# Six late weight tiles of a fused attention and mixture-of-experts kernel, loaded as 120 rows and 8 rows

## The chip, the cores and the metric

The kernel runs on one core of a Trainium2 chip. The metric is the device time of one execution in microseconds. The kernel before takes 537.62 us, the median of three runs (536.92 to 538.82).

A core has five engines with a queue of instructions each: TensorE (PE; its weight loads are listed as PEld), VectorE (DVE), ScalarE (ACT), GpSimd (POOL) and SyncE (SP). Here SP issues all transfers (DMAs); sixteen DMA engines move the bytes.

## The reference, cut to what matters

First comes attention over 8 batches, 8 heads, 576 positions and head size 64, with a bias that a small network makes of the positions. Its output, as 4608 tokens of 512 values, goes into a soft mixture of 8 experts with 4 slots each:

```python
scores = scale * np.matmul(q, k.transpose(0, 1, 3, 2)) + bias
attn = softmax(scores);  x = (attn @ v) as 4608 x 512
logits = x @ phi                       # 512 x 32
d = softmax(logits, axis=0);  slot_input = d.T @ x
for e in range(8):                     # 4 slots each
    h = np.maximum(slot_input[e] @ w1[e], 0.0)   # w1: 512 x 1024
    slot_out[e] = h @ w2[e]                      # w2: 1024 x 512
c = softmax(logits, axis=1);  out = c @ slot_out
```

All of it is in float32. The weights w1 and w2 are 32 MiB together, the output is 9 MiB.

## The kernel before, in words

Attention is worked through in 32 units (a pair of heads and a batch). For each unit TensorE makes scores, VectorE adds the bias and finds the extremes, ScalarE takes exponentials, GpSimd normalises, TensorE turns and multiplies with v. The order of all these steps on every engine stands in a long table, `ORDER`, that the host sorts by (lines 24 to 200); `step` looks up a step's place in it. A step's code then issues its instructions in that order, so each engine's queue is the table's order of its own steps. The last eight units also run the steps of the mixture (`moe`), which collect the slots' inputs; after the last step the two layers of the experts follow in a written order, and then the outputs.

The 64 weight tiles, each of 128 x 1024 floats (512 KB), are loaded by `fetch_w`: tiles 0 to 31 are of w1, tiles 32 to 63 of w2. Each call takes the next tile in `worder` and a home, a place in SBUF. Tiles 0 to 23 go to a pool of their own. The later ones go to places that attention no longer needs: the steps `wbm`, `wy`, `wqk`, `wbr`, `wv`, `wat`, `wxk`, `wv2`, `wxo` and `wat2` of the last unit give the home by pool and tag. Their places in `ORDER` set when they are issued. Tiles 36 and 37 go to "y", tile 38 to "v" and "xt" in two halves, 39 to 41 to "at", 42 and 43 to "xk", 44 again in two halves, 45 to "xo", 46 and 47 again to "at". Tiles 48 to 63 are fetched by `refetch` into the homes of tiles 0 to 13, 16 and 17 as soon as the first layer has used those (`first`, line 1019).

A transfer on SP waits for what used the place before, and for one thing more: eight semaphores serve all transfers in turn, so each transfer waits for the landing of the one that was issued eight places ahead of it.

The first layer (`first(j)`, matmuls on line 1026) uses tiles 4j to 4j+3. `hidden` and `turn_hidden` make the second layer's input. `second(k, Q, parts)` (line 1073) uses tiles 32+8k+4Q to 32+8k+4Q+3. `gather_slots` (line 1084) and `put` and `put_rest` (matmuls on line 1103) make 128 x 1024 or 128 x 512 pieces of the output, which ScalarE and VectorE copy from PSUM (line 375) into tiles `ob`, and SP sends out (lines 1117 and 1124). The order of these parts is the string at the end of `body`:

```python
for x in """S0001 T1 H0 S0101 S100 H1 G0 S101 P00 S1101 P01 S200 G1 R0 S201 P10 ...
```

Here S100 is `second(1, 0, (0,))`, which uses tiles 40 to 43, S1101 is `second(1, 1, (0, 1))`, which uses 44 to 47, and S310 with S311 use the last tiles, 60 to 63. The places of `ob` are again those of tiles that are no longer needed.

Of the kernel before, what the change touches and what calls it, by code (L numbers as in the profile page):

```python
# [231 lines left out]
def body(ctx, tc, qk, v, phi, mw1, mw2, tabh, consth, *outs):  # L232
    nc = tc.nc
    P = 128
# [15 lines left out]
    atp = ctx.enter_context(tc.tile_pool(name="atp", bufs=1))  # L250
    xp = ctx.enter_context(tc.tile_pool(name="xp", bufs=1))
# [620 lines left out]
    def fetch_w(home, n=1):  # L872
        for _ in range(n):
            i = nw[0]
            nw[0] += 1
            w, e, c, hf = worder[i]
            homeof.append(home)
            if not free:
                pool, tag = home
                if tag == "v":  # L880
                    free.append([x.tile([P, 512], F32, name="wt", tag=n, bufs=2) for x, n in ((pool, tag), (xp, "xt"))])
                elif tag == "at" and "xk" not in spare:
                    x = pool.tile([P, 2 * 9 * 320], F32, name="wt", tag=tag)
                    spare["xk"], spare["two"] = x[:, 0:5 * DM], x[:, 0:2048].rearrange("p (y n d) -> p y n d", y=2, n=2)
                    free.extend(x[:, 1024 * y - 512:1024 * y + 512].rearrange("p (n d) -> p n d", n=2) for y in (3, 4, 5))
                elif tag == "at":
                    free.extend(spare["two"][:, y] for y in range(2))
                elif tag == "xo":
                    x = pool.tile([P, 3 * S], F32, name="wt", tag=tag)
                    free.append(x[:, 0:1024].rearrange("p (n d) -> p n d", n=2))  # L890
                    spare["lg"] = x[:, 1024:1024 + 5 * P]
                else:
                    x = pool.tile([P, several.get(tag, 1), 2, 512], F32, name="wt", tag=tag, **({"bufs": 1} if tag == "br" else {}))
                    free.extend(x[:, i] for i in range(x.shape[1]))
            wt = free.pop(0)
            if w == 1:
                src = mw1[e, c * P:(c + 1) * P, :].rearrange("p (x d) -> p x d", x=2)
                if type(wt) is list:
                    for n in range(2):
                        nc.sync.dma_start(out=wt[n], in_=src[:, n])  # L900
                else:
                    nc.sync.dma_start(out=wt, in_=src)
                    wt = [wt[:, n, :] for n in range(2)]
            else:
                src = mw2[e].rearrange("p (x d) -> p x d", x=2)
                if type(wt) is list:
                    for n in range(2):
                        nc.sync.dma_start(out=wt[n], in_=src[:, n])
                else:
                    nc.sync.dma_start(out=wt, in_=src)  # L910
                    wt = [wt[:, n, :] for n in range(2)]
            wtiles[i] = wt

# [62 lines left out]
    for u, (hp, b) in enumerate(units):  # L976
        for p in range(5 - u % 2):
            rows(u, p)
        mix(u)
        if hp == NP - 1:  # L980
            moe(u)
        if u >= 2:
            step(u, "lq", lambda _, u=u: load_qk(u))
            step(u, "lv", lambda _, u=u: load_v(u))
        if 1 <= hp < NP - 1:
            for j in range(2 if u < W1N - B else 1):
                step(u, f"w{j}", lambda _: fetch_w((wp, "w")))
        if b == B - 1 and hp < NP - 1:
            for c in range(5):
                step(u, f"b{c}", lambda _, hp=hp, c=c: load_bias(hp + 1, c))  # L990
# [5 lines left out]
    for k, home in homes.items():  # L996
        step(U - 1, k, lambda _, home=home, k=k: fetch_w(home, several.get(k[1:], several.get(home[1], 1))))
# [3 lines left out]
    def refetch(*ids):  # L1001
        for i in ids:
            fetch_w(homeof[i])
# [127 lines left out]
    with tc.manual_schedule():  # L1131
# [19 lines left out]
        for x in """S0001 T1 H0 S0101 S100 H1 G0 S101 P00 S1101 P01 S200 G1 R0 S201 P10 S210 P11 S211 S300 G2 R1 P20 S301 S310 P21 S311 R2 G3 P30 P31 R3""".split():  # L1151
            i = [int(c) for c in x[1:]]
# [64 lines left out]
```

## Time and profile before

| | |
|---|---|
| median of three runs | 537.62 us (536.92 to 538.82) |
| the profiled execution's own time | 537.33 us |
| its span, from first to last instruction | 535.5 us |
| busy: PE, PEld, DVE, ACT, POOL | 517.8, 350.6, 431.3, 458.1, 217.2 us |
| DMA: bytes, mean rate | 110.14 MB, 206 GB/s |
| weight tiles of 512 KB: transfers, median time to landing | 62, 6.5 us |
| output pieces of 512 KB: transfers, median time to landing | 16, 4.6 us |

The span is divided among engines by busy time; an engine may be busy and yet not set the end. What sets the end is told by the chain of waits, which goes back from the last instruction to what released it. The time to landing of a transfer runs from its issue on SP to the last mark on its semaphore. The DMA share of a window is the mean busy share of sixteen engines; it counts a packet where it starts, so it may pass 1 a little.

### The profile page before, as it was taken

The page shows a single profiled execution, that of the slowest core. Times are in us where ns is not written, and L with a number is a line of the kernel's source. Part 1 is how long each engine was busy: PE and PEld are TensorE (multiplying, and loading weights), DVE is VectorE, ACT ScalarE, POOL GpSimd, SP SyncE. Part 2 cuts the span into 40 slices and gives each one's busy share as a digit, 9 for nine tenths or more (in the row PEclk, how much of TensorE's full clock was granted, in tenths as well). Part 3 has the DMA queues.
Part 4 walks back from the last instruction along what each step waited for, and adds up shares of the span by engine and source line. Part 5 has one row for each costly group of instructions (what it writes and reads, how often), then busy time and mean ns, then how long its engine had stood idle before and what let it go on. Part 6 is the DMA issues. An engine that isn't in the chain of part 4 may idle for free.

```text
span 535.5 us, 22642 instructions
## 1 busy us (share of the span) xinstructions
PE 517.8 (97%) x9025; PEld 350.6 (65%) x9025; DVE 431.3 (81%) x1808; ACT 458.1 (86%) x984; POOL 217.2 (41%) x317
## 2 busy tenths in 40 slices
PE   8999799999999999999999999999999999989994
PEld 6554566767767666686777667666777767653662
DVE  6898879789889888888888888888899888763343
ACT  6998899999999999999999999999888898741233
POOL 3000645565554556565454656545335341400000
PEclk9999999999999999999999999999999999999998
DMA  6689535253883535577254548635632435899988
GB/s 199 246 305 372 178 110 178 64 165 126 289 220 110 195 131 174 151 245 230 81 163 163 204 162 253 161 113 188 233 133 79 160 105 210 303 357 408 386 351 326
DMA packets 40793, 110.14 MB, mean 206 GB/s; under 512 B 5360, under 2 KB 5488, under 8 KB 40688
## 3 DMA queue, kind: packets, MB, share of 16 engines
q1 hardware_dynamic: 40688, 108.70, 59.5%
q8 instruction: 71, 1.16, 0.9%
q14 instruction: 34, 0.28, 0.2%
HBM read 81.28 MB, written 27.41 MB: 203 GB/s over the span
## 4 chain that ended last, share of the span: by engine, by line
PE 79%; DMA 6%; DVE 5%; ACT 5%; issue 2%; POOL 2%; SPq 0%; DVEq 0%; ACTq 0%; POOLq 0%
PE ps L568 23%; PE ps L425 17%; PE ps L450 14%; PE ps L444 11%; DMA bias_m<-e 3%; PE ps L1026 3%; PE ps L1073 2%; DVE y L470 2%; PE ps L1103 2%; POOL y L372 2%; ACT e L957 1%; PE ps L944 1%; PE ps L643 1%; PE ps L269 1%; DMA bias_r<-e 1%
## 5 line engine op out<-in xcount | busy, mean ns | idle before, releaser
L372 POOL TENSOR_SCALAR y<-y,rc 128x576 f32<-128x576 f32 x288 | 211.0, 749 | 224.7 <-DVE rc L489 177.3
L481 ACT ACTIVATE y<-y,mn 128x576 f32<-128x576 f32 x288 | 220.9, 776 | 7.2 <-DVE mn L470 5.7
L568 PE MATMUL ps<-at,v 64*64 64x288 f32 x2304 | 152.2, 403 | 0.0
L375 ACT COPY at<-ps 128x1024 f32<-128x1024 f32 (+3 forms) x196 | 140.0, 758 | 10.6 <-PE ps L425 7.2
L470 DVE CUSTOM_DVE_ANT_0 y<-ps,bm 128x320 f32<-128x320 f32 x256 | 115.4, 487 | 11.4 <-PE ps L444 4.6
L425 PEld LDWEIGHTS ps<-ident,y 64*128 64x128 f32 x2592 | 98.9, 138 | 34.1 <-POOL y L372 13.5
L568 PEld LDWEIGHTS ps<-at,v 64*64 64x64 f32 x2304 | 89.6, 133 | 47.2 <-ACT at L375 1.2
L470 DVE CUSTOM_DVE_ANT_0 y<-ps,bm,mn 128x256 f32<-128x256 f32 x256 | 113.9, 479 | 6.3 <-PE ps L444 1.1
L425 PE MATMUL ps<-ident,y 64*128 64x64 f32 x2592 | 106.6, 224 | 2.4 <-DVE mn L470 1.1
L450 PE MATMUL ps<-qk 64*64 64x256 f32 (+1 forms) x1280 | 92.8, 407 | 0.1
L444 PE MATMUL ps<-qk 64*128 64x320 f32 (+1 forms) x512 | 86.7, 432 | 1.4 <-DVE mn L470 1.3
L450 PEld LDWEIGHTS ps<-qk 64*64 64x64 f32 x1280 | 45.3, 132 | 28.6 <-ACT at L375 6.9
L481 ACT ACTIVATION_READ_ACCUMULATOR y<-y,mn 128x1 f32 x288 | 56.7, 197 | 0.0
L470 DVE DVE_READ_ACCUMULATOR2_ANT mn<- 128x1 f32 x576 | 48.3, 84 | 0.0
L444 PEld LDWEIGHTS ps<-qk 64*128 64x128 f32 x512 | 42.5, 189 | 7.6 <-DVE mn L470 3.0
L931 DVE TENSOR_SCALAR f<-tabw,offs 128x512 f32<-128x512 f32 (+17 forms) x107 | 39.5, 456 | 3.0 <-DMA bias_m<-e 2.8
L375 DVE COPY at<-ps 128x256 f32<-128x256 f32 (+3 forms) x60 | 35.7, 605 | 5.9 <-PE ps L425 4.7
L944 PE MATMUL ps<-f,wbd 128*32 128x512 f32 (+47 forms) x640 | 38.7, 389 | 1.3 <-ACT f L929 0.4
L944 PEld LDWEIGHTS ps<-f,wbd 128*32 128x32 f32 x640 | 20.3, 110 | 20.5 <-issue 9.0
L488 DVE TENSOR_REDUCE rc<-sm 128x2 f32<-128x4 f32 x144 | 22.0, 153 | 10.1 <-ACT y L481 9.7
L957 ACT ACTIVATE e<-ps,cons 128x591 f32<-128x591 f32 x35 | 26.3, 793 | 3.0 <-PE ps L944 3.0
L489 DVE RECIPROCAL rc<-rc 128x2 f32<-128x2 f32 x144 | 23.9, 166 | 5.0
(150 smaller groups left out, 394.7 us busy)
## 6 DMA issues: line engine op xcount, KB each, us to landing
wt<-in_moe_w_dram SPq DMA_DIRECT2D x62, 512.0 KB, 6.5
qk<-in_qk_dram SPq DMA_DIRECT2D x32, 576.0 KB, 4.2
bias_m<-e SPq DMA_DIRECT2D x32, 295.5 KB, 3.7
v<-in_v_dram SPq DMA_DIRECT2D x32, 288.0 KB, 3.3
bm<-bias_m SPq DMA_DIRECT2D x32, 288.0 KB, 5.0
out_dram<-ob SPq DMA_DIRECT2D x16, 512.0 KB, 4.6
xs<-xts SPq DMA_DIRECT2D x24, 288.0 KB, 4.0
xo<-xs SPq DMA_DIRECT2D x8, 864.0 KB, 4.7
```

The costliest lines, as they stand in the source:

```text
L372: nc.gpsimd.tensor_scalar(out=out, in0=y, scalar1=r, scalar2=1.0, op0=ALU.mult, op1=ALU.mult)
L375: (nc.vector.tensor_copy if eng else nc.scalar.copy)(out=out, in_=in_)
L425: nc.tensor.matmul(out, src[rs], ident[rs, rs], is_transpose=True, start=True, stop=True, tile_position=(64 * r, 0))
L444: nc.tensor.matmul(pss[hh].t[:, 0:nk], x[rs, S + p * P:S + (p + 1) * P], x[rs, ks], start=True, stop=True, tile_position=(64 * hh, 0))
L450: nc.tensor.matmul(pss[hh].t[64 * r:64 * r + 64, 0:nk], x[rs, q0:q0 + 64], x[rs, ks], start=True, stop=True, tile_position=(64 * hh, 64 * r))
L470: nc.vector.tensor_tensor_reduce(out=heads(hh)[:, cuts[n] // 64:cuts[n + 1] // 64], in0=d["ps", p, n][hh].read()[:, 0:nk].rearrange("a (k ...
L481: nc.scalar.activation(out=y, in_=y, func=AF.Exp, bias=d["mn", p][:, 2 + hh:3 + hh], scale=-1.0, accum_out=d["sm", p][:, hh, 0:1])
L489: nc.vector.reciprocal(out=r, in_=r)
L568: nc.tensor.matmul(d["po"][c].t[o:o + 64, 0:HALF], d["v"][rs, 64 * k:64 * k + 64], at[rs, c, 320 * k + start[c]:320 * k + start[c] + HALF] ...
L931: nc.vector.tensor_scalar(out=f, in0=tabw[:, 0:n], scalar1=off, scalar2=0.0, op0=ALU.add, op1=ALU.max)
L944: nc.tensor.matmul(x[32 * t:32 * t + 32, a:a + c1 - c0], wbd, y, start=True, stop=True, tile_position=(0, 32 * t))
L957: nc.scalar.activation(out=out, in_=x, func=AF.Copy, scale=invs[:, i:i + 1])
```

## The change

Where a whole w2 tile is loaded, tiles for the homes "xk" and "xo", and those for "at" with a number over 40, are loaded by two transfers: rows 0 to 119, and rows 120 to 127. Every row is 4 KB in DRAM and in SBUF, so the parts are 480 KB and 32 KB. All other tiles are loaded as before.

```diff
@@ -907,7 +907,9 @@
                     for n in range(2):
                         nc.sync.dma_start(out=wt[n], in_=src[:, n])
                 else:
-                    nc.sync.dma_start(out=wt, in_=src)
+                    cut = home in ((xp, "xk"), (xp, "xo")) or home == (atp, "at") and i > 40
+                    for rs in (slice(0, 120), slice(120, P)) if cut else (slice(0, P),):
+                        nc.sync.dma_start(out=wt[rs], in_=src[rs])
                     wt = [wt[:, n, :] for n in range(2)]
             wtiles[i] = wt
```

On SP, in the kernel before, these are the transfers of tiles 41 to 47 (line 908 loads tile 44 in halves). DMAHW0 to DMAHW7 are the eight semaphores of the transfers; a row's waits are for landings and for the engines that used the place before.

```order
L910 DMA wt<-in_moe_w_dram 128x1024 [waits DMAHW3_49]
L910 DMA wt<-in_moe_w_dram 128x1024 [waits DVE_49,DMAHW4_49,PE_49,Activation_49]
L910 DMA wt<-in_moe_w_dram 128x1024 [waits DMAHW5_49]
L908 DMA wt<-in_moe_w_dram 128x512 [waits DMAHW6_49]
L908 DMA wt<-in_moe_w_dram 128x512 [waits DVE_49,DMAHW7_49,PE_49,Activation_49]
L910 DMA wt<-in_moe_w_dram 128x1024 [waits DMAHW0_49]
L910 DMA wt<-in_moe_w_dram 128x1024 [waits DMAHW1_49,PE_49,Activation_49]
L910 DMA wt<-in_moe_w_dram 128x1024 [waits DMAHW2_49,PE_49,Activation_49]
```

The same place in the changed kernel, tiles 41 to 46 (line 912 is line 910 of before):

```order
L912 DMA wt<-in_moe_w_dram 120x1024 [waits DMAHW3_49]
L912 DMA wt<-in_moe_w_dram 8x1024 [waits DMAHW4_49]
L912 DMA wt<-in_moe_w_dram 120x1024 [waits DVE_49,DMAHW5_49,PE_49,Activation_49]
L912 DMA wt<-in_moe_w_dram 8x1024 [waits DMAHW6_49]
L912 DMA wt<-in_moe_w_dram 120x1024 [waits DMAHW7_49]
L912 DMA wt<-in_moe_w_dram 8x1024 [waits DMAHW0_49]
L908 DMA wt<-in_moe_w_dram 128x512 [waits DMAHW1_49]
L908 DMA wt<-in_moe_w_dram 128x512 [waits DVE_49,DMAHW2_49,PE_49,Activation_49]
L912 DMA wt<-in_moe_w_dram 120x1024 [waits DMAHW3_49]
L912 DMA wt<-in_moe_w_dram 8x1024 [waits DMAHW4_49]
L912 DMA wt<-in_moe_w_dram 120x1024 [waits DMAHW5_49,PE_49,Activation_49]
L912 DMA wt<-in_moe_w_dram 8x1024 [waits DMAHW6_49]
```

The pair of tile 47 follows, so six tiles are cut: 41, 42, 43, 45, 46 and 47. Each pair takes two of the eight semaphores, and every later transfer moves on by as many. Nothing changes its place on SP, and what follows these transfers are the sixteen whole tiles 48 to 63 and then the outputs.

On TensorE, at the start of S1101 in the kernel before (the first row is the first use of tile 44, the next three are those of tiles 45, 46 and 47):

```order
L1073 MATMUL ps<-wt,hT 32x128 [waits DMAHW6_49]
L1073 MATMUL ps<-wt,hT 32x128 [waits DMAHW0_49]
L1073 MATMUL ps<-wt,hT 32x128 [waits DMAHW1_49]
L1073 MATMUL ps<-wt,hT 32x128 [waits DMAHW2_49]
L1073 MATMUL ps<-wt,hT 32x128 x12
```

and in the changed kernel:

```order
L1075 MATMUL ps<-wt,hT 32x128 [waits DMAHW1_49]
L1075 MATMUL ps<-wt,hT 32x128 [waits DMAHW4_49,DMAHW3_49]
L1075 MATMUL ps<-wt,hT 32x128 [waits DMAHW6_49,DMAHW5_49]
L1075 MATMUL ps<-wt,hT 32x128 [waits DMAHW7_49,DMAHW0_49]
L1075 MATMUL ps<-wt,hT 32x128 x12
```

The first use of a cut tile waits for two landings in place of one. The instructions of TensorE, ScalarE, VectorE and GpSimd and their order are otherwise the same.

## Rows read from the trace of the kernel before

**Rows 1.** The page's chain that ended last, share by engine.

```profile
PE 79%; DMA 6%; DVE 5%; ACT 5%; issue 2%; POOL 2%; SPq 0%; DVEq 0%; ACTq 0%; POOLq 0%
```

**Rows 2.** Windows: window, length, busy by engine, PEclk, DMA share, GB/s.

```profile
480.00:490.00 10.00, 9.64 (x88) 3.13 (x92) 4.26 (x16) 1.63 (x4) 0.00 (x0) 1.00 0.99 379
490.00:500.00 10.00, 9.63 (x185) 5.33 (x181) 2.21 (x4) 1.86 (x3) 0.00 (x0) 1.00 1.03 408
```

**Rows 3.** Line 910 from 487 to 501 us: duration min/median/max, first and last start.

```profile
L910 SPq DMA_DIRECT2D wt<-in_moe_w_dram x11: 327/327/328, 487.8 to 500.6; - x11
...
DMA to landing us min/median/max: 10.1/10.1/10.2
```

**Rows 4.** TensorE in order of time, 519 to 524 us: start, length, instructions.

```profile
519.57 1.95 PE L1073 MATMUL ps<-wt,hT 128*32 128x128 f32 x64
```

**Rows 5.** Line 910 from 471 to 480 us.

```profile
L910 SPq DMA_DIRECT2D wt<-in_moe_w_dram x8: 328/410/679, 470.8 to 479.8; - x8
...
DMA to landing us min/median/max: 6.0/7.2/10.5
```

**Rows 6.** TensorE in order of time, 499 to 508 us.

```profile
499.25 2.83 PE L1073 MATMUL ps<-wt,hT 128*32 128x128 f32 x96 [0.37 <-ACT hT L375]
...
506.48 1.74 PE L1073 MATMUL ps<-wt,hT 128*32 128x128 f32 x56
```

**Rows 7.** Line 312, the transfers of 32 KB.

```profile
L312 SPq DMA_DIRECT2D phis<-in_moe_phi_dram x2: 964/989/1014, 4.0 to 5.0; - x2
...
DMA to landing us min/median/max: 6.3/6.7/7.1
```

**Rows 8.** SP in order of time, 470 to 506 us.

```profile
470.85 6.31 SPq L910 DMA_DIRECT2D wt<-in_moe_w_dram  x5
477.20 0.92 SPq L908 DMA_DIRECT2D wt<-in_moe_w_dram  x2
478.17 22.73 SPq L910 DMA_DIRECT2D wt<-in_moe_w_dram  x19
505.94 0.34 SPq L1117 DMA_DIRECT2D out_dram<-ob  x1
```

**Rows 9.** Waits of SP, 470 to 503 us: total us, times, longest.

```profile
SPq L910 <- DMA wt<-in_moe_w_dram: 12.0, 14, 1.7
```

**Rows 10.** Line 1117 from 526 to 530 us.

```profile
L1117 SPq DMA_DIRECT2D out_dram<-ob x4: 332/554/967, 527.3 to 529.2; - x4
...
DMA to landing us min/median/max: 3.1/4.2/4.8
```

**Rows 11.** Windows from 504 to 528 us.

```profile
504.00:508.00 4.00, 3.43 (x64) 1.84 (x65) 1.23 (x1) 1.01 (x1) 0.00 (x0) 1.00 0.98 388
508.00:512.00 4.00, 4.00 (x104) 2.63 (x96) 1.94 (x3) 1.65 (x3) 0.00 (x0) 1.00 0.60 239
512.00:516.00 4.00, 4.00 (x80) 2.18 (x76) 1.64 (x2) 1.65 (x2) 0.00 (x0) 1.00 0.91 353
516.00:520.00 4.00, 4.00 (x92) 2.65 (x84) 1.68 (x4) 1.84 (x4) 0.00 (x0) 1.00 1.02 398
520.00:524.00 4.00, 4.00 (x104) 2.84 (x96) 2.21 (x3) 1.21 (x2) 0.00 (x0) 1.00 0.96 370
524.00:528.00 4.00, 3.31 (x34) 1.45 (x28) 1.83 (x3) 2.42 (x4) 0.00 (x0) 1.00 0.87 341
```

**Rows 12.** Line 1124 from 530 to 531 us.

```profile
L1124 SPq DMA_DIRECT2D out_dram<-ob x1: 1147/1147/1147, 530.3 to 530.3; - x1
...
DMA to landing us min/median/max: 4.4/4.4/4.4
```

**Rows 13.** Line 1073 from 495 to 525 us, its one wait instruction.

```profile
L1073 PEldq EVENT_SEMAPHORE  x1: 51/51/51, 498.1 to 498.1; - x1
```

**Rows 14.** DMA queues, 470 to 503 us: packets, MB, share of 16 engines.

```profile
q8 instruction: 4, 0.07, 0.8%
```

**Rows 15.** Waits of TensorE, 496 to 530 us, all four.

```profile
PE ps L1103 <- issue: 0.6, 1, 0.6
PE ps L1103 <- ACT so L1086: 0.4, 1, 0.4
PE ps L1073 <- ACT hT L375: 0.4, 1, 0.4
PE ps L1103 <- ACT ob L375: 0.3, 1, 0.3
```

## The prediction

> **What bounds the kernel now.** I read the chain of waits first. Of the work that ended last 79% is TensorE and 6% is transfers [rows 1], so a change to transfers counts only where a transfer ends a wait or where the last transfers end the program. Next come the stretches of the tail by window. From 480 to 500 us the sixteen DMA engines are busy 0.99 and 1.03 of the time at 379 and 408 GB/s [rows 2]: the second-layer weight tiles fill them completely. There the transfers have a rate of their own. Eleven tiles are issued from 487.8 to 500.6 us, so ten steps take 12.8 us, 1.28 us for each tile of 512 KB, and every one of them lands 10.1 us after its issue [rows 3]. 10.1 is eight times 1.28 (10.2): each tile waits behind seven others, which fits the order listing, where each transfer of SP waits for the one eight places ahead of it.
>
> Does TensorE wait for these tiles? The last one issued lands at 500.6 + 10.1 = 510.7 us [rows 3]. Its first user is the second half of the 64 matmuls that start at 519.57 us and take 1.95 us [rows 4], so it is needed at about 520.5 and lies ready for 9.8 us. The six tiles that the change cuts are issued between 470.8 and 479.8 us and land 6.0 to 10.5 us later, the last by 490.3 [rows 5]. Tiles 41 to 43 are first used in the last third of the 96 matmuls from 499.25 us on, at about 501.1, and tiles 45 to 47 in the group from 506.48 us [rows 6]. Even by the worst pairing they lie ready for 10.8 us. So no weight tile ends a wait of TensorE; the transfers can only act through the outputs that queue up behind them.
>
> **The change part by part.** It issues 12 transfers in place of six, with the same bytes. The title speaks of five tiles; the order of SP shows six, since the third tile of the first "at" buffer (number 41) also meets the condition.
>
> *SP's time.* Six more issues at the median of 0.41 us in this stretch are 2.5 us, between 6 x 0.33 = 2.0 and 6 x 0.68 = 4.1 [rows 5]; the only 32 KB transfers of the run took about 1.0 us to issue, which gives 6.0 [rows 7]. I take 2.5. From 470.85 to the first output at 505.94 us SP issues nothing but weight tiles [rows 8], so only weight tiles stand behind the pairs, and in this stretch SP spends 12.0 us waiting for landings [rows 9]. The issues fit in there: 0 on the end. Without that cover they would push the last tiles by up to 6.0 us, still less than their 9.8 us of slack.
>
> *Transfers in flight.* A small transfer takes one of the eight places. Where pairs fill them, eight transfers are four tiles, 4 x 1.28 = 5.1 us of work. The shortest landing of a full-sized transfer in the tail is 3.1 us [rows 10], so the engines should not run dry. If every landing took the 6.7 us of the 32 KB transfers [rows 7], four tiles would take 6.7 instead of 5.1 us, and six tiles would lose 1.5 x 1.6 = 2.4 us. This is between 0 and 2.4 us on the weight stream; I take 0, because in a full queue bytes set the pace [rows 2, 3].
>
> *Load of single engines.* No transfer of 120 rows stands in this trace, so its spread over the engines is bounded. At best it is even and nothing changes. At worst I consider 120 rows on eight engines: 15 rows and one row of the small part make 16 where there were 8, so a tile costs 1.28 us more on these engines, 7.7 us for six. In between, the small part only puts a ninth row on engines that carry eight: an eighth of 1.28, 0.16 us for a tile and 1.0 us for six. I take 1.0 us, near the even end, because the loads of 128 rows, the nearest rows, run at full rate [rows 2]. [...]
>
> *What covers a late weight stream.* After the first output the DMA engines are not always busy. The windows from 504 to 528 us show 0.98, 0.60, 0.91, 1.02, 0.96 and 0.87 [rows 11]: 4 x (0.02 + 0.40 + 0.09 + 0 + 0.04 + 0.13) = 2.7 us idle. A stream that is up to 2.7 us late is caught up before the last outputs. 1.0 us therefore costs 0.
>
> *The end.* The last five outputs (four of 512 KB, one of 256 KB) are issued from 527.3 to 530.3 us [rows 10, 12]. The last lands at 530.3 + 4.4 = 534.7, which is 7.4 us after the first issue. Their bytes take 4.5 x 1.28 = 5.8, so 1.6 us are start, landing and unevenness between the engines. The shortest landing, 3.1 us, holds 3.1 - 1.28 = 1.8 us of such time. So hardly anything is left for a better balance to win: between 0 and 1.6 us, and I take 0.2.
>
> *TensorE's waits.* Each cut tile gives TensorE a second DMA semaphore to look at. The one row of a wait instruction on its queue in this part took 51 ns [rows 13]; six are 0.3 us on an engine that is hardly idle there. Bounds 0 and 0.3; I take 0.2.
>
> The sum is +0.2 - 0.2 = 0 on the profiled execution's 537.33 us (span 535.5, 1.8 around it). That execution lies 0.3 us below the median of 537.62, so the forecast for the median is 537.6 us.
>
> **The rivals.** *Half the engines (slower).* 120 rows go to fewer engines than 15, as in the bound above, and a tile costs these 1.28 us more. The outputs share the same engines. 7.7 us less 2.7 us of idle time are 5.0 us: 542.6. It decides from (2.7 + 1.6) / 6 = 0.72 us per tile. For it: no row shows such a shape, and the stretch has no spare engine time. Against it: the 64-row-high transfers of the start land in 6.3 to 7.1 us like others [rows 7], with no sign of a slow shape. [...]
>
> *A lagging engine is relieved (faster).* Code loading runs on the DMA engines too: 0.8% of sixteen engines over 33 us [rows 14] is 4.2 us, and if all of it falls on one engine, that engine lags, and every landing waits for it. If the 120 rows leave one engine out and it is this one, six tiles or 7.7 us are taken off it, and it no longer lags at the end. The gain is then at most the 1.6 us of the last five outputs and TensorE's one unexplained gap of 0.6 us [rows 15]: 537.6 - 2.2 = 535.4. For it: landings do wait for the slowest engine. Against it: TensorE's idle times from 496 to 530 us are four, 1.7 us in all [rows 15], and none is put down to a weight tile; no view here tells which engine lags. [...]
>
> **How the numbers follow.** The forecast, weights that stay hidden whatever their transfers look like, gets 0.70. The slower rival gets 0.12, the faster one 0.13; 0.05 stays for shifts that I don't see, 0.02 of it fast and 0.03 slow. A measurement here can tell about 0.3%, 1.6 us, from no change, so within 0.3% (536.0 to 539.2) 0.70, faster 0.15, slower 0.15. The forecast's own range is 536.0 to 539.2. The range takes half of the faster rival in and reaches towards the slower one: 535.6 to 540.6, which leaves out about 2 in 10.
>
> **What would show it.** Right: the last weight tile still lands around 511 us (within 3 us), TensorE's idle time from 496 us on stays near 1.7 us, the last five outputs still start near 527.3 and the last lands about 4.4 us after its issue. The slower rival would show as landings of the 120-row parts well over 10.5 us and DMA shares near one half in 480 to 500 us, and outputs that land later than 5 us at the end. The faster rival would show as landings under 10.1 us for the whole tiles after the pairs, and last outputs that land earlier against their issue. I am wrong if TensorE waits for a weight tile, or if SP issues its first output later than the copy that fills it.

## Result and the profile after

The changed kernel is slower: 541.3 us (538.27 to 543.67, 15 runs) against 537.58 us (535.56 to 538.82, 15 runs on the same chip). The ratio is 1.0069 [1.0053, 1.0085], or 3.7 us. The forecast was 537.6 us with a range to 540.6; it was wrong, and the slower rival came nearest.

The profiled execution of the changed kernel took 541.3 us with a span of 539.2, which is 3.7 us above the span of before. I read it in the same order as before. The chain of what ended last, 77% TensorE and 6% transfers, tells little beside [rows 1]: a loss of 0.7% hides in the rounding. The waits of TensorE from 496 us to the end (total us, times, longest) come next:

```profile
PE ps L1105 <- issue: 0.6, 1, 0.6
PE ps L1075 <- issue: 0.5, 1, 0.5
PE ps L1105 <- ACT so L1088: 0.4, 1, 0.4
PE ps L1075 <- ACT hT L375: 0.4, 1, 0.4
PE ps L1105 <- ACT ob L375: 0.3, 1, 0.3
```

The four of [rows 15] are there with the same times, and one of 0.5 us is new. It is put down to no transfer. But it is not all that TensorE loses. The same time of the clock is not the same place in the program: this execution came to the tail 0.77 us earlier, as two matmuls just ahead of the cut tiles show, first in the kernel before:

```profile
471.30 0.38 PE L823 MATMUL ps<-ident,stM 128*1 128x128 f32 x2
```

```profile
470.53 0.38 PE L823 MATMUL ps<-ident,stM 128*1 128x128 f32 x2
...
511.17 1.08 PE L1075 MATMUL ps<-wt,hT 128*32 128x128 f32 x31 [0.53 <-issue]
```

From these two to the group that uses the last tile (519.57 us in [rows 4], 520.05 below) it is 48.3 us before and 49.5 after: TensorE loses 1.2 us in the tail, between 508 and 518 us, at the place shown and at one more. In e1_columns below, which cuts no rows, it is 48.3 us again (470.09 to 518.38). One thing goes with it: the trace also records the loads of instructions, 16 KB each on queue q8, and counted from the two matmuls, the two loads that come before those places start at 38.2 and 44.3 us, where the nearest of the kernel before start at 36.2 and 40.9 and of e1_columns at 36.7 and 40.4. That these loads, behind the fuller DMA queues, hold TensorE up is not shown.

The larger loss lies behind TensorE. Now the windows of the weight stream and of the outputs, with the columns of [rows 2]:

```profile
470.00:480.00 10.00, 8.60 (x168) 5.60 (x172) 7.07 (x25) 5.65 (x11) 0.14 (x1) 1.00 1.00 316
480.00:490.00 10.00, 10.00 (x95) 3.21 (x91) 3.93 (x14) 1.36 (x3) 0.00 (x0) 1.00 1.01 234
490.00:500.00 10.00, 9.63 (x205) 5.83 (x201) 2.73 (x4) 2.07 (x4) 0.00 (x0) 1.00 1.03 351
504.00:508.00 4.00, 3.41 (x74) 2.30 (x77) 1.48 (x2) 1.01 (x1) 0.00 (x0) 1.00 1.03 411
508.00:512.00 4.00, 3.47 (x88) 2.29 (x80) 1.69 (x3) 1.65 (x3) 0.00 (x0) 1.00 1.03 407
512.00:516.00 4.00, 4.00 (x78) 2.12 (x72) 1.58 (x2) 1.58 (x2) 0.00 (x0) 1.00 1.03 414
516.00:520.00 4.00, 3.87 (x77) 2.31 (x68) 1.49 (x3) 1.43 (x4) 0.00 (x0) 1.00 1.03 413
520.00:524.00 4.00, 4.00 (x106) 2.81 (x104) 1.99 (x2) 1.55 (x2) 0.00 (x0) 1.00 1.02 405
524.00:528.00 4.00, 3.31 (x34) 1.54 (x32) 2.26 (x4) 2.06 (x5) 0.00 (x0) 1.00 1.02 409
```

The first of these windows had, in the kernel before:

```profile
470.00:480.00 10.00, 8.95 (x176) 5.67 (x168) 7.29 (x26) 5.39 (x10) 0.14 (x1) 1.00 1.00 376
```

Two things are to be seen, in the last two columns. From 470 to 500 us the DMA share is as high as before, about 1, but the rate is 316, 234 and 351 GB/s instead of 376, 379 and 408 [rows 2]. The engines are as busy as before and move less: each packet takes longer. The records of 4 KB packets, in steps of 2 us, have medians of 240 to 296 ns from 476 to 492 us, where the kernel before has 159 to 164 ns. Second, the idle time that the outputs had from 504 to 528 us, 2.7 us [rows 11], is gone: every window there is at 1.02 or 1.03.

This gives the account. The rate lost over the three windows is (60 + 145 + 57) GB/s for 10 us each, 2.62 MB; at 409 GB/s that is 6.4 us of transfer. The idle time takes up 2.7 of them, and 3.7 us remain, which is what the span gained. That this fits to 0.1 us is partly luck: counted from the two matmuls above, the span ends after 68.7 us instead of 64.2, so the tail itself is 4.5 us longer, and by the interval the medians differ by 2.8 to 4.6 us. TensorE's 1.2 us are not added to the account: no window up to 528 us has idle time of the DMA engines left, so I take it that bytes and not TensorE set the end.

Where it comes out is seen at the last four outputs, line 1119 (1117 before):

```profile
L1119 SPq DMA_DIRECT2D out_dram<-ob x4: 333/552/929, 527.7 to 529.7; - x4
...
DMA to landing us min/median/max: 7.0/7.7/7.9
```

They are issued 0.5 us later than those of [rows 10], and land 7.7 us after their issue instead of 4.2: I take it that they queue behind bytes that are still owed.

SP in order of time, from 470 us to the first output, and the last weight tiles (line 912, from 487 to 510 us):

```profile
470.08 6.86 SPq L912 DMA_DIRECT2D wt<-in_moe_w_dram  x8
476.98 0.88 SPq L908 DMA_DIRECT2D wt<-in_moe_w_dram  x2
479.47 25.51 SPq L912 DMA_DIRECT2D wt<-in_moe_w_dram  x22
506.43 4.21 SPq L1119 DMA_DIRECT2D out_dram<-ob  x4
```

```profile
L912 SPq DMA_DIRECT2D wt<-in_moe_w_dram x15: 327/328/387, 487.0 to 504.7; - x15
...
DMA to landing us min/median/max: 9.1/10.1/10.6
```

The row of 22 and that of 8 hold the pairs and the whole tiles that were 19 and 5 in [rows 8]; the first output follows 0.5 us later than there. The last weight tile is issued at 504.7 us instead of 500.6 [rows 3] and lands by 504.7 + 10.6 = 515.3 at the latest (514.8 with the median of 10.1), where the prediction's sign was 511 us within 3. Its user starts at 520.05 us:

```profile
520.05 1.95 PE L1075 MATMUL ps<-wt,hT 128*32 128x128 f32 x64
```

So still no weight tile ends a wait. Note the landings: they did not grow over [rows 3], since each transfer waits for the one eight places ahead (in the trace of before the tile issued at 478.17 us lands at 487.73, and the one eight places behind it is issued at 487.79); a slow stream shows here as later issues, not as longer landings.

### The profile page after: what moved, and what is told of

Its sections match the earlier page's. It is cut to its first block, busy times and chain, and to the rows that moved or that the text cites. A ratio compares the mean times of both kernels' runs of the same rounds, so it can differ in the third digit from the quotient of the medians.

```text
span 539.2 us, 22658 instructions
## 1 busy us (share of the span) xinstructions
PE 517.7 (96%) x9025; PEld 348.8 (65%) x9025; DVE 431.2 (80%) x1808; ACT 457.8 (85%) x984; POOL 218.5 (41%) x317
## 4 chain that ended last, share of the span: by engine, by line
PE 77%; DMA 6%; ACT 6%; DVE 5%; issue 2%; POOL 2%; SPq 1%; DVEq 0%; ACTq 0%; POOLq 0%
PE ps L568 22%; PE ps L425 16%; PE ps L450 13%; PE ps L444 10%; PE ps L1075 3%; PE ps L946 3%; PE ps L1028 3%; PE ps L1105 2%; DVE y L470 2%; DMA br<-bias_r 2%; ACT e L959 2%; DMA bias_m<-e 2%; DMA v<-in_v_dram 1%; POOL y L372 1%; ACT f L931 1%
## 5 line engine op out<-in xcount | busy, mean ns | idle before, releaser
L375 ACT COPY at<-ps 128x1024 f32<-128x1024 f32 (+3 forms) x196 | 140.0, 758 | 10.6 <-PE ps L425 7.0
L946 PE MATMUL ps<-f,wbd 128*32 128x512 f32 (+48 forms) x640 | 38.9, 389 | 1.1 <-ACT e L959 0.5
L946 PEld LDWEIGHTS ps<-f,wbd 128*32 128x32 f32 x640 | 18.9, 110 | 21.7 <-issue 9.4
```

Source lines behind the costliest of these rows:

```text
L375: (nc.vector.tensor_copy if eng else nc.scalar.copy)(out=out, in_=in_)
L946: nc.tensor.matmul(x[32 * t:32 * t + 32, a:a + c1 - c0], wbd, y, start=True, stop=True, tile_position=(0, 32 * t))
```

## Experiments

The theory after the result: a transfer of 120 rows (or its small partner) runs at about half rate on all the engines, and what this costs is lost bytes less the idle time. Rivals: the number of transfers is what costs, or the number of rows or engines, or the place of the rows. The last is theory A of the expectations: which rows a transfer has sets its rate.

**m1_shapes.** The kernel is replaced by nine stretches of 24 loads of w2 tiles each, of one shape per stretch, such as:

```diff
+        for _ in range(24):
+            x, src = at()
+            nc.sync.dma_start(out=x[32:96], in_=src[32:96])
```

> Only loads of w2 into twelve places of one tile in turn, 24 of each shape: whole tiles, rows 0-119, whole, rows 0-63, rows 32-95, rows 0-111, rows 120-127, rows 0-95, whole; zeros go out, so attention and mixture are left out. In the changed kernel the stretch 480-490 us moved 234 GB/s at a DMA share of 1.01, where before it was 379 at 0.99. [...] Theory B (count): it is the number of engines or of pieces; 120 rows are slow, rows 0-63, 32-95 and 0-111 all run at about 400. Theory C (small parts): rows 0-119 run at over 370, and the slowness belongs to the 8-row transfers.

It ran once, as did m2_ports. Windows inside the stretches, in order whole tiles; rows 0 to 119; whole; rows 0 to 63; 32 to 95; 0 to 111; 120 to 127; 0 to 95; whole (only DVE and POOL in the busy columns, then clock, DMA share, GB/s):

```profile
8.00:24.00 16.00, 0.00 (x0) 0.00 (x0) 1.00 1.03 413
45.00:70.00 25.00, 0.00 (x0) 0.00 (x0) 1.00 0.96 233
90.00:108.00 18.00, 0.00 (x0) 0.00 (x0) 1.00 1.03 409
120.00:141.00 21.00, 0.00 (x0) 0.00 (x0) 1.00 1.03 206
150.00:162.00 12.00, 0.00 (x0) 0.00 (x0) 1.00 0.96 352
175.00:200.00 25.00, 0.00 (x0) 0.00 (x0) 1.00 1.03 235
216.00:223.00 7.00, 0.00 (x0) 0.00 (x0) 1.00 0.44 58
234.00:255.00 21.00, 0.00 (x0) 0.00 (x0) 1.00 1.03 239
270.00:288.00 18.00, 0.00 (x0) 0.00 (x0) 1.00 1.03 409
```

The 120 rows alone run at 233 GB/s, 0.57 of a whole tile's rate, with no small part beside them: the small parts are not what costs most. Rows 0 to 63 and rows 32 to 95 are as many rows and bytes, at 206 and 352 GB/s, 0.50 and 0.86 of a whole tile's rate: not how many rows decides, but which. Theory A gave rows 0 to 119 at 200 to 250 GB/s, rows 0 to 63 at about 200 and rows 32 to 95 at about 400. The rate is near the 234 GB/s of the changed kernel from 480 to 490 us, where other shapes are mixed in. One rival isn't parted from this: in every stretch the rows taken from DRAM are the same as the rows filled in SBUF, so the runs don't tell whether the place in SBUF or the place in DRAM matters.

**m2_ports.** Why 120 rows are slow was open, so the same kernel ran with other rows (`x[32:92]`, `x[4:124]`, `x[0:128:2]`, `x[0:32:4]` and more).

> This kernel leaves out attention and the mixture: it only loads second-layer weight tiles, nine stretches of 24 transfers: whole; rows 32 to 91; rows 4 to 123; every second row (64); every fourth row of 0 to 31 (8); rows 120 to 127; rows 0 to 59; rows 0 to 119; whole. Open is why 120 rows load at 233 GB/s and rows 32 to 95 at 352. [...] Rival 'fifteen engines': transfers on 15 engines are slow as such: rows 32 to 91 at about 230 or less. [...]

Windows inside the nine stretches, in the order of the expectation:

```profile
8.00:22.00 14.00, 0.00 (x0) 0.00 (x0) 1.00 1.02 412
34.00:44.00 10.00, 0.00 (x0) 0.00 (x0) 1.00 0.96 392
55.00:85.00 30.00, 0.00 (x0) 0.00 (x0) 1.00 0.96 227
105.00:117.00 12.00, 0.00 (x0) 0.00 (x0) 1.00 0.95 347
122.00:130.00 8.00, 0.00 (x0) 0.00 (x0) 1.00 0.20 51
138.00:143.00 5.00, 0.00 (x0) 0.00 (x0) 1.00 0.52 52
152.00:166.00 14.00, 0.00 (x0) 0.00 (x0) 1.00 0.97 199
182.00:205.00 23.00, 0.00 (x0) 0.00 (x0) 1.00 0.97 222
236.00:250.00 14.00, 0.00 (x0) 0.00 (x0) 1.00 1.03 409
```

Rows 32 to 91 run at 392 GB/s at a DMA share of 0.96, rows 0 to 119 at 222 with 0.97, and whole tiles at 412 and 409 with 1.02 and 1.03. By these shares, as an estimate, both shapes leave about one engine of sixteen idle; so fifteen engines as such are not slow. Rows 4 to 123 are slow (227) and rows 0 to 59 (199). Every second row ran at 347 GB/s, where I had expected 205 to 240, and every fourth row of 0 to 31 needed 16 x 0.20 / (51 GB/s / 4 KB) = 0.26 us a packet, where I had expected 0.16; rows 120 to 127, as many rows, need 16 x 0.52 / (52 GB/s / 4 KB) = 0.66 by the same reckoning. So again it matters which rows, not only how many; but what I held of them before this run does not fit, and no run shows how the rows of a transfer slow it. The cause inside the 120-row transfer stays open. That such a transfer is slow at both starts tried, row 0 and row 4 (222 and 227 GB/s), and on its own, is shown.

**e1_columns.** The same six tiles in two halves by columns, all 128 rows in each: as many transfers, as many semaphores.

```diff
-                    for rs in (slice(0, 120), slice(120, P)) if cut else (slice(0, P),):
-                        nc.sync.dma_start(out=wt[rs], in_=src[rs])
+                    for xs_ in (slice(0, 1), slice(1, 2)) if cut else (slice(0, 2),):
+                        nc.sync.dma_start(out=wt[:, xs_], in_=src[:, xs_])
```

> The same six tiles in two transfers each, but cut by columns: 128 rows x 512 twice. The number of transfers, of SP's issues and of places taken is that of the changed kernel, and all rows are there. Theory A: 537.6 us as before, ratio within 0.998 to 1.002, windows 480-490 us at about 380 GB/s. Theory of the places in flight (twice as many transfers leave fewer bytes in flight): slower as the changed kernel, about 541.

537.92 us against 537.01: ratio 1.0010 [0.9997, 1.0022]. The windows from 470 to 500 us have the rates of before, but for the first:

```profile
470.00:480.00 10.00, 8.60 (x162) 5.28 (x162) 6.68 (x25) 5.25 (x10) 0.14 (x1) 1.00 0.96 353
480.00:490.00 10.00, 10.00 (x96) 3.21 (x91) 3.93 (x14) 1.36 (x3) 0.00 (x0) 1.00 1.00 377
490.00:500.00 10.00, 9.63 (x217) 6.14 (x213) 2.73 (x4) 2.07 (x4) 0.00 (x0) 1.00 1.02 408
```

Six more issues on SP, six more waits and fewer tiles in flight cost nothing that can be told from no change.

**e2_rows64 and e3_rows112.** The cut at another row.

```diff
-                    for rs in (slice(0, 120), slice(120, P)) if cut else (slice(0, P),):
+                    for rs in (slice(0, 64), slice(64, P)) if cut else (slice(0, P),):
```

> The same six tiles cut at row 64: rows 0-63 and 64-127. [...] Theory B (an odd number of engines, one engine left out, small parts): sixteen engines with four rows each, 537.6 us as before.

541.77 us against 537.01: 1.0084 [1.0059, 1.0109]; theory A gave 541 to 543 us, with windows of 200 to 250 GB/s from 480 to 490. The windows lose (376 - 297) + (379 - 227) + (408 - 320) = 319 GB/s over 10 us, 3.2 MB or 7.8 us; less 2.7 us are 5.1, and 4.8 were measured:

```profile
470.00:480.00 10.00, 7.85 (x151) 4.86 (x147) 5.80 (x22) 5.39 (x10) 0.14 (x1) 1.00 0.91 297
480.00:490.00 10.00, 9.18 (x112) 3.48 (x104) 4.83 (x19) 0.94 (x3) 0.00 (x0) 1.00 1.02 227
490.00:500.00 10.00, 10.00 (x165) 4.75 (x158) 2.19 (x3) 1.96 (x3) 0.00 (x0) 1.00 1.02 320
```

There is no 8-row transfer here, and the loss is at least as large. That 5.1 meets 4.8 so closely is partly luck: in this trace TensorE also waits for a load that was issued at 464.9 us, before the first cut tile, and for which it does not wait in the kernel before:

```profile
PE ps L425 <- DMA xo<-xs: 1.6, 1, 1.6
```

```diff
-                    for rs in (slice(0, 120), slice(120, P)) if cut else (slice(0, P),):
+                    for rs in (slice(0, 112), slice(112, P)) if cut else (slice(0, P),):
```

> The same six tiles cut at row 112: rows 0-111 and 112-127. Sixteen engines can share both evenly (7 rows and 1 row). [...] Theory B (uneven load of the engines): 537.6 us as before.

539.32 us against 537.01: 1.0053 [1.0034, 1.0073], 2.3 us; theory A gave 538.5 to 541 us. Its windows have 324, 259 and 401 GB/s: 1.8 MB or 4.4 us lost, less 2.7 are 1.7. The trace is of the fastest of its six runs, 537.79 us, whose span is only 0.2 us above that of before.

**e4_middle.** The rows that were fast, in the kernel: 32 to 95, then the outer quarters.

```diff
-                    for rs in (slice(0, 120), slice(120, P)) if cut else (slice(0, P),):
+                    for rs in (slice(32, 96), slice(0, 32), slice(96, P)) if cut else (slice(0, P),):
```

> The same six tiles in three transfers each: rows 32-95, rows 0-31, rows 96-127. More transfers than in the changed kernel (18 for six tiles), each on sixteen engines. Theory A (place): half of the bytes run at full rate, as rows 32-95 did by themselves, half of them slowly, so about half of what the cut at 64 lost, 3.9 us of the stream, less the 2.7 us in which the DMA engines idle after the first output: 1.2 us slower than before, 537.0 + 1.2 = 538.2 us (537.5 to 539.5). Theory of the pieces (each further transfer costs): 18 transfers cost more than 12, so over 541 us.

538.52 us against 537.25, 1.3 us. One of its twelve runs took 1289 us, for a reason that isn't known; the median of the other eleven is 538.18, and their ratio 1.0031 [1.0008, 1.0054]. It has three transfers to a tile where e2_rows64 has two, and by the ratios costs about 0.4 of it: once more the rows, not the count.

**e5_three and e6_twelve.** The cut of after on three tiles and on twelve. If the idle time covers the first 2.7 us, three tiles cost little and twelve more than twice what six do; if each tile costs its share, it is proportional.

```diff
-                    cut = home in ((xp, "xk"), (xp, "xo")) or home == (atp, "at") and i > 40
+                    cut = i in (41, 42, 43)
```

> Only tiles 41, 42 and 43 are cut at row 120; 45, 46 and 47 are whole again. By the account of lost bytes (six cut tiles lose 2.6 MB against before, 6.4 us at 409 GB/s, and 2.7 us of that are caught up after the first output) three tiles lose 3.2 us and 0.5 us is left: 537.5 us, ratio 1.001 (0.999 to 1.003). If every cut tile costs the end its share of the measured 3.7 us, three cost 1.9 us: 538.9, ratio 1.0035.

538.09 us against 537.25: 1.0016 [0.9995, 1.0037], 0.9 us. The interval holds both expectations; this run tells nothing apart.

```diff
-                    cut = home in ((xp, "xk"), (xp, "xo")) or home == (atp, "at") and i > 40
+                    cut = i in (41, 42, 43, 45, 46, 47, 48, 49, 50, 51, 52, 53)
```

> Twelve tiles are cut at row 120: 41 to 43 and 45 to 53. By the account of lost bytes 12.8 us less 2.7 us: 10.1 us slower, 547 us (545 to 549). If every cut tile costs the same 0.6 us: 7.4 us, 544.4 us. The last weight tile then lands at about 523 us, 2 us after its first use, so TensorE should wait for it; the outputs that queue behind the weights end no later for that.

546.88 us against 537.25: 1.0176 [1.0151, 1.0201], 9.6 us, and 8.1 to 10.8 by the interval. Proportional would be 7.4, the account 10.1: the account fits better. But twice the measured 3.7 us is 5.7 to 9.1 by its interval, which reaches into this one, so the proportional cost is not excluded. And the account put the lost bytes at twice those of six tiles, 12.8 us; in this trace the windows from 470 to 508 us lose 4.3 MB, 10.4 us, which less 2.7 are 7.7, where the span is 8.7 us longer. The expected wait of TensorE did not come: the last tile is issued at 509.9 us and lands by 520.5, its user starts at 521.75, and no wait is put down to a weight tile. The rate stays low as long as cut tiles are under way, and the first outputs fall into it:

```profile
490.00:500.00 10.00, 9.63 (x169) 4.95 (x165) 1.70 (x3) 1.86 (x3) 0.00 (x0) 1.00 0.96 256
...
504.00:508.00 4.00, 4.00 (x84) 2.28 (x73) 1.22 (x1) 1.20 (x3) 0.00 (x0) 1.00 0.97 310
```

**e7_early.** Six early tiles (8 to 13, of w1) cut, the late ones whole. These are loaded during attention, where the engines have idle time on the mean.

```diff
-                    nc.sync.dma_start(out=wt, in_=src)
+                    for rs in (slice(0, 120), slice(120, P)) if i in (8, 9, 10, 11, 12, 13) else (slice(0, P),):
+                        nc.sync.dma_start(out=wt[rs], in_=src[rs])
```

> Six tiles of w1, numbers 8 to 13, are cut at row 120, and the late ones are whole again. These are issued between about 175 and 290 us, where the DMA engines are busy 0.40 to 0.67 of the time and the tiles are needed 200 us later. Theory A with the account of lost bytes: the packets are as slow, but there is idle time enough: ratio 1.000 (0.998 to 1.002). If the slow packets delayed the other loads of that stretch (q, k, v and bias tiles of attention), over 1 us slower.

539.5 us against 537.25: 1.0035 [1.0017, 1.0053]; the expectation was missed. One place is seen in the trace. A cut tile is issued at 236.9 us, just ahead of the loads of the bias, which unit after unit need. DMA issues from 236 to 246 us (count, KB each, median us to landing), in this kernel and then in the kernel before:

```profile
br<-bias_r SPq DMA_DIRECT2D x4, 144.0 KB, 8.1
```

```profile
br<-bias_r SPq DMA_DIRECT2D x4, 144.0 KB, 6.3
```

and VectorE's waits from 242 to 256 us, in the same order:

```profile
DVE y L470 <- DMA br<-bias_r: 1.5, 1, 1.5
DVE y L470 <- PE ps L450: 1.0, 1, 1.0
```

```profile
DVE y L470 <- DMA br<-bias_r: 0.6, 1, 0.6
```

The bias lands 1.8 us later and VectorE waits 0.9 us more for it, and 1.0 us more for what hung on that. In the traces of the changed kernel and of the six experiments above on late tiles, all early tiles are whole; there the bias lands after 5.6 to 6.7 us and the wait for it is at most 1.2 us. So 8.1 and 1.5 us stand out, but a part of these differences comes without any early cut. This trace also has a wait of TensorE that the kernel before has not, and that e2_rows64 has too, with whole early tiles:

```profile
PE ps L425 <- DMA xo<-xs: 1.1, 1, 1.1
```

So the idle time of the engines on the mean did not cover these tiles; that the cause is the bias, which queues behind a cut tile, fits the trace but is not shown.

## Why the prediction was wrong, point by point

- **What bounds the kernel.** Right for the waits: TensorE waits for no weight tile in either kernel, and the loss comes out at the outputs behind the tiles. Not only there, though: TensorE itself is 1.2 us later in the tail. The prediction also says that the title speaks of five tiles; it speaks of six, the number that the sums use.
- **SP's time, transfers in flight.** Taken as 0 each, and e1_columns, which has both and none of the row cuts, gives 1.0010 [0.9997, 1.0022].
- **Load of single engines.** This step failed. It was sized at 1.0 us, between 0 and 7.7, and measured 6.4 us (2.62 MB at 409 GB/s). I counted how many rows an engine has to carry, and chose "near the even end, because the loads of 128 rows, the nearest rows, run at full rate". What the runs showed in its place is that a packet is slower when the rows of a transfer lie wrongly: the records of 4 KB packets have a median near 160 ns in the whole stretch before, and 240 to 296 ns from 476 to 492 us after, in steps of 2 us. How many rows an engine got was, as an estimate from the marks, not off by much: in the trace of after, the landing of a 120-row transfer leaves 15 marks spread in time on its semaphore (issued at 470.93 us; one mark at 471.54 and fifteen from 477.28 to 479.46), and that of 8 rows leaves 8 (issued at 471.47 us; one mark at 471.97 and eight from 477.54 to 479.73).
- **Evidence that was misread.** Against the slower rival I held that the 64-row-high transfers of the start land in 6.3 to 7.1 us like others [rows 7]. The landing of two transfers of 32 KB gave no rate of a stream; in m1_shapes rows 0 to 63 turned out slower than every taller shape, at 206 GB/s. With no row on the shape, the step had no ground to prefer the even end.
- **The cover.** Right: 2.7 us of idle time [rows 11] was taken up first. 6.4 - 2.7 = 3.7 us, the measured loss; e2_rows64 (5.1 against 4.8), e3_rows112 (1.7 against 2.3) and e6_twelve follow the same account within one to two microseconds, no closer, as said at each.
- **The end and TensorE's waits.** The gain of up to 1.6 us by a better balance did not come: the last four outputs of 512 KB land 3.1 to 3.9 us later against their issue ([rows 10]: 3.1 to 4.8; after: 7.0 to 7.9), and their issue is 0.5 us later by the clock and 1.2 us counted from the start of the tail. On TensorE 1.2 us were added where I took 0.2 and bounded it by 0.3; six looks at a semaphore are not what it was, since e1_columns has them too and loses nothing. The cause stays open.
- **The rivals.** "Half the engines" named the right place and nearly the right size, 542.6 us, with 7.7 us where 6.4 was measured. Its mechanism is not the one: the 15 marks above fit fifteen engines and not eight. That fifteen is what 120 rows get, or that they leave an engine out, was my assumption in both rivals; no row of before shows it. Its sign "DMA shares near one half" was wrong: a slow packet counts as busy, and the share was 1.01 at 234 GB/s. Its sign "landings well over 10.5 us" was wrong as well, its sign "outputs later than 5 us" right. The faster rival did not show: single whole tiles land after 9.1 us instead of 10.1, but their median is still 10.1, and none of the last outputs lands sooner. Landings do wait for a last mark that comes late: in the trace of before the tile issued at 478.17 us has fifteen of its sixteen marks by 484.95 us and the last at 487.73. But no run shows which engine lags.

## What to carry to other kernels

Here a transfer's shape had a rate of its own, 233 GB/s for 120 rows and 409 to 413 for whole tiles, and the DMA share, 0.96 and 1.03, did not show it: read GB/s beside the share, and measure a new shape in a stretch of its own before cutting a tile by rows; a cut by columns that keeps all 128 rows cost nothing here (ratio 1.0010). Price a slower stream as bytes lost over the full rate, take off the idle time behind it, and look where the rest comes out, here in the landing of the last outputs. Idle time on the mean was not cover for the early tiles of e7_early (1.0035): look for what is needed and queues behind the slow transfer. And compare two traces from a common instruction, not by the clock: here 0.77 us of the difference was hidden by the clock.

## What was not expected of the hardware

- Rows 0 to 119, 0 to 111 and 0 to 95 load at 233 (222 in m2_ports), 235 and 239 GB/s in m1_shapes, whole tiles of 128 rows at 409 to 413.
- The same number of rows at another start differs by a factor: 64 rows from 0 at 206 GB/s and from 32 at 352 (m1_shapes); 60 rows from 0 at 199 and from 32 at 392 (m2_ports).
- Eight rows from 120 on run at 52 GB/s with a DMA share of 0.52 in m2_ports and at 58 with 0.44 in m1_shapes. By share and rate that is 0.66 and 0.50 us a 4 KB packet, three to four times the 0.16 us of a packet of a whole tile (413 GB/s with 1.03).
- The issue on SP depends on the rows too: in m1_shapes a median of 328 ns for 128 rows, 465 ns for rows 0 to 63 and 591 ns for rows 32 to 95.
